# Attention followed by two dense layers on one Trainium2 core: decoding of the weights at another rate and on another DMA queue, token splits two slices a step, two output buffers, earlier first loads

## The chip, the cores and the metric

The kernel runs on one core of one Trainium2 chip. The metric is the device time of one execution in microseconds (us). TensorE is PE in the profile (PEld is its weight load), VectorE is DVE, ScalarE is ACT, GpSimd is POOL and SyncE is SP; SP only issues DMAs here.

## The reference

Batch 4, 12 heads, 448 positions, head size 64; the weights of the dense layers arrive as float64.

```python
scores = scale * q @ k.T                          # per head
scores = einsum('bhij,hg->bgij', scores, w_pre)   # heads mixed
attn = softmax(scores)                            # over the last axis
attn = einsum('bhij,hg->bgij', attn, w_post)      # heads mixed again
x = (attn @ v).transpose(0, 2, 1, 3).reshape(1792, 768)
h = x @ w_in                                      # 768 x 2048
g = where(h > 0, h, exp(min(h, 0)) - 1)
out = g @ w_out                                   # 2048 x 768
```

## The kernel before

**Attention.** Each batch is cut into 4 blocks of query positions; a block is 9 or 12 tiles of 10 positions by 12 heads (120 rows). The program is written in 92 steps `j` of up to two tiles each. In step `j` PE makes the scores of step `j+2` (tile `s`, L208), on some steps two head pairs of `q·k` for a block ahead (tile `qk`, L189; copied to `st` and sent by SP into `raw`), on some steps two head pairs of attention times values for a finished block (L259), and then the second mixing of heads of step `j` (tile `t`, L234). DVE takes the maximum `nm` (L210), the inverse sum `rz` (L220, L221), half of the `st` copies and the output copy `x` (L271); ACT makes the exponential `p` (L212) and copies `t` to `at` (L245); POOL scales the mixing matrix `wz` (L225). The results of L259 and of L234 share two PSUM banks, so the second `t` of a step has to wait until the copy `x` has emptied the bank that L259 used. A block's `x` is collected in one buffer (`xp`, one buffer) and stored to DRAM by SP after its third copy (`xd<-x`, L275).

**Decoding the weights.** `Weights.run` is a generator over 48 pieces of 128x512 weights, 24 for each layer. A piece is loaded (`w<-in`, 512 KB, L53), made into float32 by four DVE instructions (L67, L70, L76, L79 into `c`) and one ACT square (`sq`, L74, beside L70; L79 needs it), and stored to DRAM scratch (`s<-c`, L83). One call of `dec.step` goes on to the next `yield`, so a piece takes four steps; the store of a piece, the load of the piece after the next and L67 of the next come in one step. There are two `w`, two `c` and one `sq` buffers. Loads and stores are all issued by POOL.

**The dense layers.** `Moe` runs over two halves of the tokens (two chunks of 448 each, `u` = 0 and 1). The first layer has 16 slices `f` of 128 outputs: per slice and chunk 18 matmuls (L446) into `h`, then `elu`: DVE L454, ACT exponential and tanh (L456, L457), DVE L459 and L460. `keep` splits the result `g` into a high part on ACT (`gh`, L464) and a low part on POOL (`gl`, L465). The second layer has 6 row blocks `m` of two jobs `e`, each 48 matmuls (L514). Every slice and job first loads its weights from scratch (`load_w`, SP, two ahead, three buffers) and splits the next slice's (`split_w`: ACT `hi`, L395, then POOL `lo`, L396). The tokens are split in the same way: ACT `xh` (L408) and DVE `xl` (L409).

**Where decoding stands.** In attention one or two steps from `j = 6` on, in the first half's first layer one step per slice (at `u = 0`), in its second layer eight per job until the pieces are done. All engines run their instructions in the order in which the program was written; nothing reorders them.

Of the kernel before, what the change touches and what calls it, by code (L numbers as in the profile page):

```python
# [27 lines left out]
NC = DM // 128  # L28
PW = 512
EPS = 1e-9  # L30
LATE = 6


def f32(ap):
    return ap.bitcast(F32)
# [71 lines left out]
def attention(ctx, tc, qd, kd, vd, wpre, wpost, xd, dec, moe):  # L107
    nc = tc.nc
# [5 lines left out]
    def pool(name, on=ctx, side="left", **kw):  # L114
        return on.enter_context(tc.tile_pool(name=name, side=side, **kw))
# [3 lines left out]
    small = pool("small", bufs=5)  # L119
    atp = pool("at", bufs=2)  # L120
    vp = pool("v", bufs=NP + 2)
    xp = pool("x", bufs=1)
    rawp = pool("raw", bufs=2)
    kp = pool("kp", op_ctx, "right", bufs=NP + 1)
    qp = pool("qp", op_ctx, "right", bufs=2)
# [17 lines left out]
    N = len(steps)  # L143
# [30 lines left out]
    def load_v(b, hp):  # L174
        vs[b, hp] = vp.tile([128, NJ, 128], F32, tag="v", name="v")[:CJ]
        nc.gpsimd.dma_start(out=vs[b, hp], in_=vd[b, hp])
# [129 lines left out]
    def plan(j, f):  # L306
        work.setdefault(max(j, -LOOK), []).append(f)

    for n in range(1, NBL):
        b, i = blocks[n]  # L310
# [11 lines left out]
    for n in range(NBL):  # L322
        b, i = blocks[n]
# [4 lines left out]
                for hp in (2 * u, 2 * u + 1):  # L328
                    plan(j + 1, lambda b=b + 1, hp=hp: load_v(b, hp))
    for hp in range(NP):  # L330
        plan(hp + 2, lambda hp=hp: load_v(0, hp))

    sc, nz = {}, {}
    for j in range(-LOOK, N + 3):
        if j == N - 7:
            op_ctx.close()
            moe.begin()
        if j == N:
            moe.first()
        if 0 <= j + LOOK < N:  # L340
            sc[j + LOOK] = scores(*steps[j + LOOK])
        for n, u in units.get(j, ()):
            got = [qk(n, hp) for hp in (2 * u, 2 * u + 1)]
            for w in range(2):
                keep_qk(n, 2 * u + w, got[w])
        if j + LOOK - 1 in sc:
            nz[j + LOOK - 1] = norm(*sc.pop(j + LOOK - 1))
        for n, u in avs.get(j, ()):
            for w in range(2):
                av(n, 2 * u + w)  # L350
            keep_av(n, u)
        if j in nz:
            keep_post(*steps[j], post(nz.pop(j)))
        if LATE <= j < N:
            dec.step(1 + (j % 3 == 0))
        for f in work.get(j, ()):
            f()
        if N - 5 <= j < N:
            moe.ahead(j - (N - 5))


class Moe:


    def __init__(self, ctx, tc, xd, s1, s2, dec, outT):
        self.ctx, self.tc, self.nc = ctx, tc, tc.nc
        self.xd, self.dec, self.outT = xd, dec, outT

        self.jobs = [(s, lo, n) for half in range(2)
                     for s, lo, n in [(s1, f * NC, NC) for f in range(NF)]  # L370
                     + [(s2, 8 * e, 8) for e in range(2 * NC)]]
        self.w, self.x, self.banks = {}, {}, 0

    def pool(self, name, side="left", **kw):
        return self.ctx.enter_context(self.tc.tile_pool(name=name, side=side, reuse_waits="tile", **kw))
# [27 lines left out]
            self.nc.sync.dma_start(out=f32(xl[:, :, i0:i0 + m]), in_=self.xd[c][i][:, :, :m])  # L403
        self.x[c] = xh, xl

    def split_x(self, c, k):
        xh, xl = self.x[c]
        self.nc.scalar.copy(xh[:, k, :], f32(xl[:, k, :]))  # L408
        self.nc.vector.tensor_sub(xl[:, k, :], f32(xl[:, k, :]), f32(xh[:, k, :]))  # L409

    def begin(self):
# [4 lines left out]
        self.load_w(0)  # L418
        self.load_x(1)
        self.load_w(1)  # L420

    def ahead(self, step):
        if step < 4:
            for k in range(3):
                self.split_x(step // 2, step % 2 * 3 + k)
        if 1 <= step <= 2:
            self.split_w(step - 1)

    def first(self):
        self.h = [self.up(0, u) for u in range(2)]  # L430
# [16 lines left out]
                n += 1  # L447
        return h

    def elu(self, h, decode):  # L450
        nc = self.nc

        g = self.ep.tile([128, S], F32, tag="g", name="g", bufs=3)
        nc.vector.tensor_scalar_min(g, h, 0.0)  # L454
        e = self.ep.tile([128, S], F32, tag="e", name="e")
        nc.scalar.activation(e, g, AF.Exp)  # L456
        nc.scalar.activation(g, g, AF.Tanh, scale=0.5)  # L457
        self.dec.step(decode)
        nc.vector.scalar_tensor_tensor(g, e, 1.0, g, op0=ALU.add, op1=ALU.mult)  # L459
        nc.vector.tensor_max(g, g, h)  # L460
        return g
# [4 lines left out]

    def run(self):
        nc = self.nc
        self.ep = self.pool("ep", bufs=2)
        gp = self.pool("g", bufs=1)  # L470
        op = self.pool("op", bufs=2)
        self.ps.append(self.pool("ps1", bufs=1, space=PSUM))
        self.gh = [gp.tile([128, 2, S], F32R, name=f"gh{f}") for f in range(NF)]
        self.gl = [gp.tile([128, 2, S], F32R, name=f"gl{f}") for f in range(NF)]
        i = 0
        for half in range(2):
            last = None
            for f in range(NF):
                self.load_w(i + 2)
                if i:  # L480
                    self.split_w(i + 1)
                for u in range(2):
                    g = self.elu(self.up(i, 2 * half + u) if i else self.h[u], 1 - u)
                    if last:
                        self.keep(*last)
                    last = g, f, u
                del self.w[i]
                i += 1
            for m in range(NC):
                y = [self.bank("y") for u in range(2)]  # L490
                for e in range(2):
                    self.load_w(i + 2)
                    self.split_w(i + 1)
                    if last:
                        self.keep(*last)
                        last = None
                    if half == 0:
                        if m == e == 0:
                            self.load_x(2)
                            self.load_x(3)  # L500
                        if m > 1:
                            for k in range(3):
                                t = (m - 2) * 6 + e * 3 + k
                                if t < 2 * NC:
                                    self.split_x(2 + t // NC, t % NC)
                        self.dec.step(8)
                    wh, wl = self.w.pop(i)
                    i += 1
                    for u in range(2):
                        for k in range(8):  # L510
                            f = e * 8 + k
                            ks = slice(k * 128, (k + 1) * 128)
                            for n, (w, g) in enumerate(((wh, self.gh), (wl, self.gh), (wh, self.gl))):
                                nc.tensor.matmul(  # L514
                                    y[u], w[:, ks], g[f][:, u, :],
                                    start=f == 0 and n == 0, stop=f == NF - 1 and n == 2)
                for u in range(2):
                    c = 2 * half + u
                    o = op.tile([128, S], F32, tag="o", name="o")
                    nc.scalar.copy(o, y[u])  # L520
                    nc.sync.dma_start(out=self.outT[m * 128:(m + 1) * 128, c * S:(c + 1) * S], in_=o)
# [46 lines left out]
```

## Time and profile before

| what | value |
|---|---|
| median of 3 runs | 992.41 us (986.24 to 999.28) |
| the profiled execution | 990.38 us |
| its span, first to last instruction | 988.6 us |
| PE busy | 931.9 us (94%) |
| DVE / ACT / POOL busy | 531.7 / 471.3 / 453.7 us |
| mean granted TensorE clock | 0.981 |
| DMA | 136.30 MB, mean 138 GB/s |

The profiled execution spends 1.8 us outside its span. A busy share is a mean over stages with different limits: attention lies at 0 to 488 us, the first half's two layers at 488 to 621 and 621 to 753, the second half at 753 to 985. What PE waits for is therefore looked up stage by stage.

### The profile page before, as it was taken

The numbers are of one execution on the slowest core, as the hardware profiler recorded it, in microseconds if no ns is written. First come the engines' busy times: TensorE is split into PE (matmuls) and PEld (weight loads), VectorE is DVE, ScalarE is ACT, GpSimd is POOL, SyncE is SP. The second block draws the span as 40 slices with busy tenths as digits, with TensorE's granted clock in tenths as the row PEclk, the third lists the DMA queues.
The fourth block names the chain that finished last, engine by engine and source line by source line (L and its number), as shares of the span: only waits on it lengthen the run. The fifth ranks groups of instructions, "written<-read, shape, count | busy, mean of one in ns | idle before, by whom it ended". The sixth has DMA issues, their size and how long they took to land.

```text
span 988.6 us, 17106 instructions
## 1 busy us (share of the span) xinstructions
PE 931.9 (94%) x6216; PEld 771.9 (78%) x6216; DVE 531.7 (54%) x957; ACT 471.3 (48%) x988; POOL 453.7 (46%) x496
## 2 busy tenths in 40 slices
PE   4979999899999899999799999998899999999998
PEld 1657777677777677777688888887799999999997
DVE  3647666576667566765558888766611555410000
ACT  3746666556556555665535554423322555532111
POOL 2347446564457444543435555543341556543210
PEclk8989999999999999999999999999999999999999
DMA  5566456664677456757112222855532121212220
GB/s 169 174 193 214 137 182 197 199 188 138 189 224 217 125 156 189 227 169 218 63 64 89 82 86 85 225 189 188 189 117 67 50 64 48 69 58 92 74 80 29
DMA packets 76633, 136.30 MB, mean 138 GB/s; under 512 B 22894, under 2 KB 51890, under 8 KB 76550
## 3 DMA queue, kind: packets, MB, share of 16 engines
q1 hardware_dynamic: 60598, 80.41, 26.1%
q0 software_dynamic: 15408, 53.89, 17.8%
q8 instruction: 50, 0.82, 0.3%
q10 hardware_dynamic: 544, 0.92, 0.2%
q14 instruction: 33, 0.27, 0.1%
HBM read 72.86 MB, written 23.62 MB: 98 GB/s over the span
## 4 chain that ended last, share of the span: by engine, by line
PE 65%; DVE 14%; DMA 11%; issue 5%; ACT 3%; POOL 1%; SPq 1%; ACTq 0%; DVEq 0%; POOLq 0%
PE y L514 16%; PE h L446 13%; PE t L234 13%; PE s L208 12%; PE t L259 6%; PE qk L189 6%; DMA xd<-x 6%; DVE g L459 3%; DMA w<-in 3%; DVE c L79 2%; DVE g L454 2%; DVE xl L409 2%; DVE c L70 1%; DVE c L76 1%; DVE c L67 1%
## 5 line engine op out<-in xcount | busy, mean ns | idle before, releaser
L225 POOL TENSOR_SCALAR wz<-wb,rz 120x120 f32<-120x120 f32 x180 | 127.5, 716 | 182.2 <-DVE rz L221 159.5
L234 PEld LDWEIGHTS t<-wz,p 120*112 120x112 f32 x1440 | 159.3, 178 | 41.5 <-issue 31.7
L234 PE MATMUL t<-wz,p 120*112 120x120 f32 x1440 | 171.1, 271 | 14.9 <-DVE x L271 14.1
L396 POOL TENSOR_TENSOR lo<-lo,hi 128x768 fp32r<-128x768 f32 (+1 forms) x56 | 116.8, 2085 | 125.8 <-ACT hi L395 125.8
L208 PE MATMUL s<-raw,wa 120*120 120x448 f32 x360 | 156.4, 557 | 14.8 <-DMA raw<-st 7.8
L210 DVE TENSOR_REDUCE nm<-s 120x1 f32<-120x448 f32 x180 | 111.8, 624 | 96.8 <-PE s L208 86.9
L212 ACT ACTIVATE p<-s,nm 120x448 f32<-120x448 f32 x180 | 114.2, 635 | 85.6 <-DVE nm L210 81.1
L514 PE MATMUL y<-gh,lo 128*128 128x448 f32 x384 | 142.2, 370 | 9.2 <-POOL lo L396 9.2
L446 PE MATMUL h<-xh,lo 128*128 128x448 f32 x384 | 141.9, 370 | 6.6 <-POOL lo L396 6.6
L245 ACT COPY at<-t 112x480 f32<-112x480 f32 x180 | 96.4, 560 | 104.6 <-PE t L234 104.2
L514 PE MATMUL y<-gh,hi 128*128 128x448 f32 x384 | 141.2, 368 | 0.2
L446 PE MATMUL h<-xh,hi 128*128 128x448 f32 x384 | 141.2, 368 | 0.0
L514 PE MATMUL y<-gl,hi 128*128 128x448 f32 x384 | 141.2, 368 | 0.0
L446 PE MATMUL h<-xl,hi 128*128 128x448 f32 x384 | 140.8, 367 | 0.0
L465 POOL TENSOR_TENSOR gl<-g,gh 128x448 fp32r<-128x448 f32 x64 | 77.0, 1204 | 125.8 <-ACT gh L464 125.5
L208 PEld LDWEIGHTS s<-raw,wa 120*120 120x120 f32 x360 | 60.4, 188 | 51.7 <-issue 43.4
L456 ACT ACTIVATE e<-g 128x448 f32<-128x448 f32 x64 | 37.0, 579 | 123.7 <-DVE g L454 123.7
L459 DVE SCALAR_TENSOR_TENSOR g<-e,g 128x448 f32<-128x448 f32 x64 | 55.4, 865 | 63.6 <-ACT g L457 63.6
L259 PEld LDWEIGHTS t<-at,v 112*64 112x64 f32 x1536 | 74.2, 136 | 18.4 <-issue 13.7
L514 PEld LDWEIGHTS y<-gh,lo 128*128 128x128 f32 x384 | 73.4, 191 | 16.9 <-POOL lo L396 11.9
L259 PE MATMUL t<-at,v 112*64 112x120 f32 (+1 forms) x1536 | 84.1, 262 | 1.4 <-ACT at L245 1.4
L446 PEld LDWEIGHTS h<-xh,lo 128*128 128x128 f32 x384 | 72.4, 189 | 16.4 <-POOL lo L396 10.7
(49 smaller groups left out, 1255.7 us busy)
## 6 DMA issues: line engine op xcount, KB each, us to landing
raw<-st SPq DMA_DIRECT2D x144, 210.0 KB
w<-in POOLq DMA_DIRECT2D x48, 512.0 KB, 5.4
lo<-s SPq DMA_DIRECT2D x80, 256.0 KB
s<-c POOLq DMA_DIRECT2D x48, 256.0 KB, 3.5
raw<-st SPq DMA_DIRECT2D x42, 157.5 KB
q<-in POOLq DMA_DIRECT2D x15, 360.0 KB, 5.8
v<-in POOLq DMA_DIRECT2D x24, 224.0 KB, 5.2
out<-o SPq DMA_DIRECT2D x24, 224.0 KB
```

The source lines that it names most:

```text
L208: nc.tensor.matmul(ps[:RH, :S], wa, raws[n][:RH, t, :], start=True, stop=True)
L210: nc.vector.tensor_reduce(nm, ps[:RH, :S], op=ALU.max, axis=AX.X, negate=True)
L212: nc.scalar.activation(p, ps[:RH, :S], AF.Exp, bias=nm, scale=1.0, accum_out=z[:, i:i + 1])
L225: nc.gpsimd.tensor_scalar_mul(wz, wb, rz[:, i:i + 1])
L234: nc.tensor.matmul(ps[:CJ, c * RH:(c + 1) * RH], p[:, c * CJ:(c + 1) * CJ], wz, start=True, stop=True,)
L245: nc.scalar.copy(ats[n][:, :, t, :], ps[:CJ, :NJ * RH].rearrange("p (c n) -> p c n", c=NJ))
L259: nc.tensor.matmul(ps[hh * 64:(hh + 1) * 64, w * m:(w + 1) * m].rearrange("p (t r) -> p t r", r=R), vs[blocks[n][0], hp][:, c, hh * 64:(hh ...
L396: self.nc.gpsimd.tensor_sub(lo_, f32(lo_), f32(hi_))
L446: self.nc.tensor.matmul(h, w[:, ks], x[:, k, :], start=n == 0, stop=n == 3 * NC - 1)
L459: nc.vector.scalar_tensor_tensor(g, e, 1.0, g, op0=ALU.add, op1=ALU.mult)
L465: self.nc.gpsimd.tensor_sub(self.gl[f][:, u, :], g, f32(self.gh[f][:, u, :]))
L514: nc.tensor.matmul(y[u], w[:, ks], g[f][:, u, :], start=f == 0 and n == 0, stop=f == NF - 1 and n == 2)
```

## The change

The decoding starts at step 12 instead of 6, runs alternately one and two steps instead of one, one, two, and stops six steps before attention's end. In the first layer it takes a step for each of the two chunks of a slice instead of one per slice, in the second layer seven steps a job instead of eight (and whatever is left in the last row block); from the dense layers on its DMAs are issued by SP instead of POOL. The token split is cut in two calls, the high parts (`high_x`, ACT) and one step later the low parts (`low_x`, DVE), two slices of 128 rows at a time instead of three. The first loads of the dense layers are written 10 steps before attention's end instead of 7. `x` gets a second buffer. The values of the first batch are loaded two head pairs at a time at steps 4, 6 and 8 instead of one at each of steps 2 to 7.

```diff
-LATE = 6
+LATE = 12
...
-    xp = pool("x", bufs=1)
+    xp = pool("x", bufs=2)
...
     for hp in range(NP):
-        plan(hp + 2, lambda hp=hp: load_v(0, hp))
+        plan(hp // 2 * 2 + 4, lambda hp=hp: load_v(0, hp))
...
-        if j == N - 7:
+        if j == N - 10:
             op_ctx.close()
             moe.begin()
         if j == N:
+            moe.low_x(2 * NC - 2)
             moe.first()
...
+        if N - 5 <= j < N:
+            moe.low_x(2 * (j - N + 5))
         for n, u in avs.get(j, ()):
...
-        if LATE <= j < N:
-            dec.step(1 + (j % 3 == 0))
+        if LATE <= j < N - 6:
+            dec.step(1 + j % 2)
         for f in work.get(j, ()):
             f()
-        if N - 5 <= j < N:
-            moe.ahead(j - (N - 5))
+        if N - 6 <= j < N:
+            moe.high_x(2 * (j - N + 6))
+        if N - 4 <= j < N - 2:
+            moe.split_w(j - N + 4)
...
+    def high_x(self, t, n=2):
+        for t in range(t, t + n):
+            xh, xl = self.x[self.c0 + t // NC]
+            self.nc.scalar.copy(xh[:, t % NC, :], f32(xl[:, t % NC, :]))
+
+    def low_x(self, t, n=2):
+        for t in range(t, t + n):
+            xh, xl = self.x[self.c0 + t // NC]
+            r = xl[:, t % NC, :]
+            self.nc.vector.tensor_sub(r, f32(r), f32(xh[:, t % NC, :]))
...
-        self.dec.step(decode)
+        self.dec.step()
...
     def run(self):
         nc = self.nc
+        self.dec.queue = nc.sync
...
-                    g = self.elu(self.up(i, 2 * half + u) if i else self.h[u], 1 - u)
+                    g = self.elu(self.up(i, 2 * half + u) if i else self.h[u])
...
                         if m == e == 0:
+                            self.c0 = 2
                             self.load_x(2)
                             self.load_x(3)
-                        if m > 1:
-                            for k in range(3):
-                                t = (m - 2) * 6 + e * 3 + k
-                                if t < 2 * NC:
-                                    self.split_x(2 + t // NC, t % NC)
-                        self.dec.step(8)
+                        t = ((m - 2) * 2 + e) * 2
+                        if 2 <= t < 2 * NC + 2:
+                            self.low_x(t - 2)
+                        if 0 <= t < 2 * NC:
+                            self.high_x(t)
+                        self.dec.step(7 if m < NC - 1 else 64)
```

How the instructions stand on DVE over two slices of the first half's first layer, from a slice whose `u = 0` carries L79 on; `g` is the activation, `c` a piece being decoded. Before:

```order
L454 TENSOR_SCALAR g<-h 128x448
L79 SCALAR_TENSOR_TENSOR c<-sq,c 128x512
L459 SCALAR_TENSOR_TENSOR g<-e,g 128x448
L460 TENSOR_TENSOR g<-g,h 128x448
L454 TENSOR_SCALAR g<-h 128x448
L459 SCALAR_TENSOR_TENSOR g<-e,g 128x448
L460 TENSOR_TENSOR g<-g,h 128x448
L454 TENSOR_SCALAR g<-h 128x448
L67 TENSOR_SCALAR c<-w 128x512
```

In the changed kernel the lines of `elu` are five higher:

```order
L459 TENSOR_SCALAR g<-h 128x448
L76 SCALAR_TENSOR_TENSOR c<-w,c 128x512
L464 SCALAR_TENSOR_TENSOR g<-e,g 128x448
L465 TENSOR_TENSOR g<-g,h 128x448
L459 TENSOR_SCALAR g<-h 128x448
L79 SCALAR_TENSOR_TENSOR c<-sq,c 128x512
L464 SCALAR_TENSOR_TENSOR g<-e,g 128x448
L465 TENSOR_TENSOR g<-g,h 128x448
L459 TENSOR_SCALAR g<-h 128x448
L67 TENSOR_SCALAR c<-w 128x512
```

A decoding instruction now stands in both chunks of each slice, between the first and the second instruction of `elu`; L76 and L67 take turns at `u = 0`, L79 and L70 at `u = 1`.

POOL around the start of the first half's second layer, before; `lo` is the weight split of the coming job, `s` the scratch of a piece:

```order
L396 TENSOR_TENSOR lo<-lo,hi 128x1024
L465 TENSOR_TENSOR gl_6054<-g,gh_6038 128x448
L83 DMA s_8_105<-c 128x512
L53 DMA w<-in 128x1024
L83 DMA s_9_106<-c 128x512
L53 DMA w<-in 128x1024
L396 TENSOR_TENSOR lo<-lo,hi 128x1024
```

In the changed kernel POOL has only `gl` and `lo` there, and these stand on SP, among the loads of that layer's weights (`lo<-s`) and of the second half's tokens (`xl<-xd`):

```order
L393 DMA lo<-s_4_101 128x512
L393 DMA lo<-s_5_102 128x512
L408 DMA xl<-xd_0_65 128x6x90
...
L408 DMA xl<-xd_3_72 128x6x118
L83 DMA s_11_108<-c 128x512
L53 DMA w<-in 128x1024
L83 DMA s_12_109<-c 128x512
L53 DMA w<-in 128x1024
L393 DMA lo<-s_6_103 128x512
```

The stores and loads of the decoding have left POOL's row of splits and stand behind the eight token loads on SP, ahead of the next job's weights.

DVE at attention's end, from the fifth-last step's output copy on. Before:

```order
L271 COPY x<-t 128x240
L79 SCALAR_TENSOR_TENSOR c<-sq,c 128x512
L67 TENSOR_SCALAR c<-w 128x512
L409 TENSOR_TENSOR xl<-xl,xh 128x448 x3
L210 TENSOR_REDUCE nm<-s 120x1 x2
L220 TENSOR_SCALAR rz<-z 120x2
L221 RECIPROCAL rz<-rz 120x2
L70 SCALAR_TENSOR_TENSOR c<-w,c 128x512
L409 TENSOR_TENSOR xl<-xl,xh 128x448 x3
```

In the changed kernel, from the inverse sum ahead of that copy on:

```order
L221 RECIPROCAL rz<-rz 120x2
L421 TENSOR_TENSOR xl<-xl,xh 128x448 x2
L271 COPY x<-t 128x240
L210 TENSOR_REDUCE nm<-s 120x1 x2
L220 TENSOR_SCALAR rz<-z 120x2
L221 RECIPROCAL rz<-rz 120x2
L421 TENSOR_TENSOR xl<-xl,xh 128x448 x2
L210 TENSOR_REDUCE nm<-s 120x1 x2
```

The decoding instructions are gone from these steps, and two low parts of tokens stand ahead of the output copy where three stood behind it.

## Rows read from the trace of the kernel before

**Rows 1.** Busy time by stage: the stretch and its length, then for each engine busy us and (x instructions), the granted clock of PE, the DMA share, and GB/s.

```profile
0.00:100.00 100.00, 80.17 (x564) 53.87 (x566) 56.26 (x119) 53.79 (x124) 47.77 (x70) 0.91 0.61 188
100.00:458.00 358.00, 348.44 (x3052) 259.83 (x3049) 229.75 (x514) 218.91 (x519) 182.94 (x255) 0.99 0.60 183
458.00:488.00 30.00, 22.12 (x206) 17.76 (x205) 19.72 (x41) 18.62 (x42) 13.86 (x16) 0.98 0.32 106
488.00:621.00 133.00, 126.40 (x673) 113.00 (x672) 98.68 (x110) 62.16 (x110) 65.36 (x52) 0.99 0.27 82
621.00:753.00 132.00, 122.64 (x578) 111.40 (x577) 67.17 (x80) 36.26 (x58) 50.84 (x46) 0.96 0.56 174
753.00:985.00 232.00, 232.00 (x1153) 216.08 (x1151) 60.11 (x96) 81.00 (x135) 92.94 (x59) 1.00 0.19 64
```

**Rows 2.** Who waited for whom: us in total, times, longest us. The first row is DVE's over the whole span; then PE's in 100 to 460 us, in 460 to 490 (four rows), in 500 to 621 and in 621 to 753.

```profile
DVE x L271 <- DMA xd<-x: 19.3, 8, 4.0
...
PE t L234 <- DVE x L271: 9.6, 7, 2.8
...
PE t L234 <- DVE x L271: 4.5, 3, 2.2
PE t L259 <- ACT at L245: 1.4, 1, 1.4
PE s L208 <- ACT p L212: 1.1, 1, 1.1
PE t L234 <- POOL wz L225: 0.8, 1, 0.8
...
PE h L446 <- POOL lo L396: 6.6, 11, 1.1
...
PE y L514 <- POOL lo L396: 9.2, 7, 2.0
```

**Rows 3.** Instructions in order of time: start us, duration us, engine and line, then in brackets the idle time of the engine before it and what ended it. One output copy on DVE, and PE behind it.

```profile
178.11 0.34 DVE L271 COPY x<-t 128x180 f32<-128x180 f32 x1 [3.79 <-DMA xd<-x]
...
178.60 1.04 PE L234 MATMUL t<-wz,p 120*112 120x120 f32 x8 [2.85 <-DVE x L271]
```

**Rows 4.** Busy time in two of the stretches in which PE's clock was at half, columns as in rows 1; the others are 326.7 to 330.1, 487.1 to 490.5, 623.6 to 627.0, 688.5 to 691.9 and 702.1 to 705.5 us, each 3.4 us at 0.50.

```profile
63.80:70.70 6.90, 3.04 (x4) 1.12 (x4) 4.06 (x8) 3.25 (x8) 4.32 (x6) 0.51 0.47 167
179.90:183.30 3.40, 3.40 (x11) 2.12 (x10) 1.59 (x5) 1.35 (x4) 1.94 (x2) 0.50 0.61 203
```

**Rows 5.** In order of time, the first decoding instruction on DVE, and PE.

```profile
65.39 0.43 DVE L67 TENSOR_SCALAR c<-w 128x512 int32<-128x512 int32 x1 [8.21 <-DMA w<-in]
...
67.66 3.24 PE L208 MATMUL s<-raw,wa 120*120 120x448 f32 x4 [5.91 <-ACT p L212]
```

**Rows 6.** PE's first attention times values, in order of time; then the landing of a value load (issued at 51.2 us, in step 4's place) and of the 23 loads of pieces issued from 95 to 426 us, from issue to landing.

```profile
55.33 1.46 PE L259 MATMUL t<-at,v 112*64 112x90 f32 x32
...
DMA to landing us min/median/max: 6.2/6.2/6.2
...
DMA to landing us min/median/max: 4.2/6.5/8.6
```

**Rows 7.** In order of time, PE in the last steps of attention, two of its waits.

```profile
465.79 1.05 PE L234 MATMUL t<-wz,p 120*112 120x120 f32 x8 [1.63 <-DVE x L271]
...
477.75 2.83 PE L234 MATMUL t<-wz,p 120*112 120x120 f32 x24 [2.16 <-DVE x L271]
```

**Rows 8.** In order of time, the first half's first layer: DVE over one slice and the first half of the next, then POOL.

```profile
540.56 2.28 DVE L79 SCALAR_TENSOR_TENSOR c<-sq,c 128x512 f32<-128x512 f32 x1
542.77 1.58 DVE L459 SCALAR_TENSOR_TENSOR g<-e,g 128x448 f32<-128x448 f32 x1
...
544.92 0.62 DVE L454 TENSOR_SCALAR g<-h 128x448 f32<-128x448 f32 x1
546.85 0.62 DVE L459 SCALAR_TENSOR_TENSOR g<-e,g 128x448 f32<-128x448 f32 x1 [1.31 <-ACT g L457]
...
548.05 0.62 DVE L454 TENSOR_SCALAR g<-h 128x448 f32<-128x448 f32 x1
...
553.60 0.62 DVE L454 TENSOR_SCALAR g<-h 128x448 f32<-128x448 f32 x1
...
542.46 1.40 POOL L465 TENSOR_TENSOR gl<-g,gh 128x448 fp32r<-128x448 f32 x1 [0.17 <-ACT gh L464]
```

**Rows 9.** In order of time, the first half's second layer: a load of a piece and a weight split on POOL, ACT, DVE (the low parts of three token slices as one row); last the 14 loads of pieces of that layer, with the first and last start, and their landing.

```profile
658.12 0.53 POOL L53 DMA_DIRECT2D w<-in  x1
662.93 2.43 POOL L396 TENSOR_TENSOR lo<-lo,hi 128x1024 fp32r<-128x1024 f32 x1 [4.28 <-ACT hi L395]
...
661.23 0.68 ACT L74 ACTIVATE sq<-w 128x512 f32<-128x512 f32 x1 [7.75 <-DMA w<-in]
661.81 1.04 ACT L395 CAST hi<-lo 128x1024 fp32r<-128x1024 f32 x1
...
661.71 0.69 DVE L70 SCALAR_TENSOR_TENSOR c<-w,c 128x512 int32<-128x512 int32 x1
...
686.38 3.49 DVE L409 TENSOR_TENSOR xl<-xl,xh 128x448 fp32r<-128x448 f32 x3 [0.97 <-ACT xh L408]
...
L53 POOL DMA_DIRECT2D w<-in x14: 533/533/536, 634.1 to 708.6; - x14
...
DMA to landing us min/median/max: 4.3/4.9/5.9
```

More of the change, by code (lines that the diff above doesn't have):

```diff
@@ L371, in __init__ @@
                      + [(s2, 8 * e, 8) for e in range(2 * NC)]]
-        self.w, self.x, self.banks = {}, {}, 0
+        self.w, self.x, self.c0, self.banks = {}, {}, 0, 0
     def pool(self, name, side="left", **kw):
@@ L404, in load_x @@
         self.x[c] = xh, xl
[L406 to L409, printed above, removed]
+    def high_x(self, t, n=2):
[7 more added lines that the diff above has]
+            self.nc.vector.tensor_sub(r, f32(r), f32(xh[:, t % NC, :]))
     def begin(self):
@@ L420, in begin @@
         self.load_w(1)
-    def ahead(self, step):
-        if step < 4:
-            for k in range(3):
-                self.split_x(step // 2, step % 2 * 3 + k)
-        if 1 <= step <= 2:
-            self.split_w(step - 1)
     def first(self):
@@ L448, in up, with elu @@
         return h
-    def elu(self, h, decode):
+    def elu(self, h):
         nc = self.nc
@@ L498, in run @@
                         if m == e == 0:
+                            self.c0 = 2
                             self.load_x(2)
                             self.load_x(3)
-                        if m > 1:
-                            for k in range(3):
-                                t = (m - 2) * 6 + e * 3 + k
-                                if t < 2 * NC:
-                                    self.split_x(2 + t // NC, t % NC)
-                        self.dec.step(8)
+                        t = ((m - 2) * 2 + e) * 2
[4 more added lines that the diff above has]
+                        self.dec.step(7 if m < NC - 1 else 64)
                     wh, wl = self.w.pop(i)
```

## The prediction

> **What bounds the kernel now.** I read the stages first, then PE's waits in each, then the instructions around the largest. PE is the bound nearly everywhere [rows 1]: it is busy 348 of 358 us in the middle of attention and all 232 us of the second half. There 1153 matmuls take 232 us, 0.201 us each, which is the floor of a dense matmul: a slice of the first layer (36) needs 7.25 us, a job of the second (48) 9.66 us. So only idle time of PE and time at half clock can be won. Five places have some. In attention's middle PE waits 9.6 us for the output copy `x` [rows 2], and that copy had itself waited for the store `xd<-x`, 19.3 us in 8 waits. At the start PE stands 5.91 us because DVE, in order, stood 8.21 us at the first piece of weights [rows 5]. In 460 to 490 us it waits 7.8 us in six pieces [rows 2]. In the first half's layers it waits for POOL's `lo`, 6.6 and 9.2 us [rows 2], and at 621 to 753 us the granted clock is 0.96 [rows 1]. The larger waits are followed by 3.4 us at 0.50, the lower level of 1.2 GHz [rows 4]; each such stretch costs 1.7 us beside the wait. The second half has nothing to win. The sum is made against the profiled 990.38 us (988.6 of span and 1.8 around it), 2 us under the median.
>
> **Second `x` buffer.** Seven of the eight DVE waits lie in blocks where the store of the block before had not landed when its buffer was to be refilled, one of them just ahead of the last steps. With two buffers the store waited for is a whole block older, six steps of some 5 us (92 in 488), against waits of at most 4.0 us [rows 2, 3]: they all go. PE's share is at most 9.6 us in seven pieces and 1.63 us at 465.79 [rows 2, 7], 11.2 us, and two half-clock stretches, at 179.9 and 326.7 us [rows 4], 3.4 us: 14.6 us. What is late next is seen in the steps without such a wait, in which PE shows none from 100 to 460 us. I take **-13**; ends -14.6 and -7 (half of the waits turning into waits for `nm` or `rz`).
>
> **Start of decoding.** Before, the step that issued the first load also held the first L67, so DVE waited the whole landing. Now step 12 issues the load and step 13 uses it, a step of some 5 us later. With the later landings of 4.2 to 8.6, median 6.5 us [rows 6], DVE waits about 1.5 us, at most 3.6. Of the 8.21 us of before PE felt 5.91, so it had 2.3 us in hand: residue 0 to 1.3 us, taken as 0.5. Saved are 5.91 and, of the 3.04 us busy at half clock, 1.5 [rows 4, 5]: 7.4 us. But the values come later. The load in step 4's place was issued at 51.2 us and landed after 6.2 us [rows 6]; that place now holds the first two head pairs, the first landing at 57.4 and the second one transfer of 224 KB later (1.2 us at 188 GB/s, rows 1), at 58.6, and PE wants them at 55.33 and half of its 1.46 us later [rows 6]: it stands about 2.5 us. Steps 6 and 8 load for steps 8 and 10 in the same manner, behind a `ql` or `kl` on POOL; with fewer transfers around, the piece's loads being gone from there, they cost 0 to 2 and 0 to 1 us. Together +3.5, ends 1 and 7. The start is worth -7.4 + 0.5 + 3.5, **-3.5**; ends -7 and +1.
>
> **End of attention.** Without the store's wait there are 7.8 - 1.6 = 6.2 us of waits and the 1.7 us of half clock behind them. They come from DVE: three low parts and a decoding instruction a step, and the weight split on POOL, which holds up `rz` and `wz` (2.16 us, rows 7). Decoding leaves; two low parts instead of three remain, but now ahead of the output copy that frees PE's bank, 1.2 us on three steps; both weight splits remain. I take half, **-4**; ends -8 and +1. The first loads three steps earlier gain nothing by themselves, since no wait of PE or ACT for them is in these rows; they wait on SP for the last `raw` stores, and nothing is queued behind them there until the next `xd<-x`. The decoding done by attention's end is 111 steps against 115 (before 86 + 29, now 74 + 37).
>
> **First layer, first half.** A slice takes 8.0 us (from the L454 some 0.5 us ahead of L79 to the L454 at 548.05), not 7.25, and it is DVE that sets it: its instructions run with one gap only [rows 8]. At `u = 0` the decoding instruction runs into POOL's `lo` (2.28 us) and L459 into `gl` (1.58), 4.9 us for the half; at `u = 1` DVE waits 1.31 us for ACT's tanh, 3.1 us for the half. The added step falls into this gap: POOL's `gl` ended at 543.86, and an undisturbed decoding instruction takes 0.69 us [rows 9]. So 16 more steps cost nothing as long as POOL is idle there. What POOL no longer issues saves some 0.7 us on every fourth slice (5.55 us from 548.05 to 553.60 against 4.9): -2.6. The square `sq` now stands at `u = 1` on every second slice, ahead of `gh`, `hi` and so `lo`, 0.68 us each on ACT, at most 8 x 0.68 = 5.4, of which I take 3.6, since `lo` then meets DVE at another point. **+1**; ends -3 and +5. SP's store now waits there for `c`, and what is queued behind it is weights wanted two slices later.
>
> **Second layer, first half.** 132 us against a floor of 12 x 9.66 = 115.9: 16 us lost. The loop: ACT's square waits for a piece's load (7.75 us idle) and holds `hi` behind it, POOL's `lo` follows, PE waits [rows 9]. With 8 steps a job there are two loads a job, each issued only after the last L79: landing 4.9 us, four instructions 2.7 us (0.43 and three of 0.69, with their gaps), one of them held by `lo` for some 2 us, store and load issue 1.1 us, so 10.7 us a job; with the three `xl` in between (3.49 us) 14 us. Now 51 steps remain instead of 63 (16 went into the first layer's gaps), 7 a job, 1.75 pieces: 10.7 x 0.875 = 9.4 us, and two `xl` whose high part was made a job before add 1.2 us in two or three jobs, which the lead of two jobs hides. The pace is then PE's 9.66 us. The first job's loss, 1.8 us of waiting for its longer `lo` and 1.7 us of half clock, stays. **-12**; ends -16 and 0.
>
> Sum: -13 - 3.5 - 4 + 1 - 12 = -31.5, so **959 us**.
>
> **The rivals.** (1) *The step at `u = 1` meets POOL after all.* `gl` ends 1.6 us before that step's place, and the square shifts it by 0.68; if it shifted past, both halves of a slice would be as long as the first, 9.8 us: 16 x 1.8 = +28, 986 us. With halves of 5.55 us, the longest seen [rows 8], it is 16 x 3.1 = +49, **1007 us, slower than before**. For it: DVE is the bound there. Against: POOL lost work. It decides once POOL is over 1.6 us late. 0.08 and 0.03. The Trainium skill (SBUF — State Buffer, Who interferes with whom) has DVE's and GpSimd's shared port as a lock held for a whole instruction, whoever comes first; by that rule the gap is free only while POOL rests, as the 2.28 us beside 0.69 agree. (2) *SP's queue.* The loads of the second half's tokens, 8 transfers of together 2.75 MB, now stand ahead of the pieces' loads; at some 200 GB/s (174 in the mean of the stage, rows 1) that is 13 us. Before, the first such load was issued at 634.1 us, 13 us into the layer, and landed near 640 [rows 9], so the queue may well be empty by then. If the pieces do come 13 us later than that, a job still has 9.66 us for 3.5 us of `hi` and `lo`; some 7 us reach PE, with a half clock 9: 968 us, 0.1. The Trainium skill (DMA: Bandwidth & Descriptors, Queues, rings and completion order) says that an engine takes turns between queue rows but works one row's ring in order; by that rule the full 13 us would be queued, where POOL's own row shared with them. No row here shows a piece's load on SP. (3) *The copies keep waiting*, if the stores, not the buffer, are what is late: 959 + 13 = 972. The waits end at a landing of the block before, which speaks against it. 0.04.
>
> **How the numbers follow.** Forecast 0.75, the three rivals 0.11, 0.1 and 0.04. All five terms at their good ends would give 941, at their bad ends 991; as unrelated errors (1.6, 3.5, 4, 4 and 4 one way, 6, 4.5, 5, 4 and 12 the other, squares added) they give 951 and 975. With rivals 2 and 3 inside and rival 1 outside, and the good side widened for a better first layer, the range is 945 to 976. 2% of 992.4 is 20 us, about what a measurement here tells from no change, so faster means below 972.6: 0.83. Same 0.14, slower 0.03 (rival 1's long form).
>
> **What would show it.** DVE's waits for `xd<-x` gone and no half clock near 180 and 327 us; a wait of PE for values near 55 to 58 us; no 8 us wait at the first piece; a slice of the first layer still at 8 us with decoding in both halves; in the second layer jobs at 9.7 us after the first, and no `hi` behind a late square. Wrong would be slices of 9 us or more, and jobs 1 to 3 waiting for pieces on SP.

## The result, and the profile after

The changed kernel takes 949.74 us (median; 947.24 to 958.08), the kernel before in the same session 995.85 (986.24 to 1002.01): a ratio of 0.958, 95% interval 0.947 to 0.969. The forecast was 959 us. The profiled execution took 947.56 us with a span of 945.8; before it was 990.38 and 988.6. The matmuls are the same, and PE's busy share rose to 97%.

The page's head, the engines' busy time, PE's granted clock in 40 slices, and the chain that ended last, which now stays on PE for 81% of the span (65% before):

```profile
span 945.8 us, 17070 instructions
...
PE 915.8 (97%) x6216; PEld 764.4 (81%) x6216; DVE 528.7 (56%) x957; ACT 470.5 (50%) x988; POOL 435.6 (46%) x456
...
PEclk8999999999999999999999999999999999999999
...
PE 81%; DVE 8%; DMA 3%; issue 3%; ACT 3%; POOL 1%; ACTq 0%; POOLq 0%; DVEq 0%
```

The stages, columns as in [rows 1]: start, attention's middle and end, first layer and second layer of the first half, second half.

```profile
0.00:100.00 100.00, 81.76 (x606) 55.85 (x606) 51.38 (x115) 54.30 (x127) 44.56 (x67) 0.95 0.56 172
100.00:437.00 337.00, 335.85 (x2956) 250.76 (x2954) 235.55 (x515) 215.21 (x511) 184.06 (x255) 1.00 0.65 198
437.00:466.40 29.40, 26.09 (x258) 21.09 (x257) 17.24 (x38) 20.22 (x46) 14.29 (x16) 1.00 0.41 121
466.40:595.00 128.60, 124.78 (x675) 112.47 (x675) 102.89 (x127) 66.29 (x117) 66.68 (x45) 1.00 0.33 104
595.00:710.20 115.20, 115.20 (x578) 108.13 (x577) 61.55 (x69) 32.93 (x52) 33.08 (x15) 1.00 0.57 179
710.20:942.20 232.00, 232.00 (x1153) 216.10 (x1151) 60.09 (x96) 80.99 (x135) 92.95 (x59) 1.00 0.19 64
```

Beside [rows 1] the middle's idle time of PE went from 10 us to 1.2, the second layer's from 9.4 to none, and the granted clock is 1.00 from 100 us on. Cut at the first matmul of each layer and at the end of the last matmul, the stages are:

| | attention | first layer | second layer | second half |
|---|---|---|---|---|
| before, us | 487.6 | 133.2 | 132.1 | 232.1 |
| after, us | 466.4 | 128.6 | 115.2 | 232.1 |
| difference | -21.2 | -4.6 | -16.9 | 0 |

PE's waits, as in [rows 2]: in 50 to 100 us; in 100 to 440; in 440 to 466.4 (two rows); in 480 to 595. In 595 to 710 us there is none, and DVE's waits for `xd<-x` are gone from the whole span.

```profile
PE t L259 <- DMA v<-in: 4.0, 3, 2.1
...
PE t L234 <- DVE x L271: 1.1, 3, 0.5
...
PE t L234 <- POOL wz L225: 2.3, 2, 1.3
PE t L259 <- ACT at L245: 1.0, 1, 1.0
...
PE h L451 <- POOL lo L401: 3.6, 6, 1.1
```

At the start, in order of time: the wait for the piece on DVE that stood at 8.21 us [rows 5], and PE's three waits for values.

```profile
96.27 0.43 DVE L67 TENSOR_SCALAR c<-w 128x512 int32<-128x512 int32 x1 [2.36 <-DMA w<-in]
...
57.51 0.84 PE L259 MATMUL t<-at,v 112*64 112x90 f32 x16 [2.10 <-DMA v<-in]
58.74 0.84 PE L259 MATMUL t<-at,v 112*64 112x90 f32 x16 [0.40 <-DMA v<-in]
...
78.27 1.58 PE L259 MATMUL t<-at,v 112*64 112x90 f32 x32 [1.53 <-DMA v<-in]
```

DVE in the first layer, over one slice and most of the next, as in [rows 8]: the decoding instruction and the second instruction of `elu` (L464; L459 before) of each chunk. At `u = 1` both are undisturbed, 0.68 and 0.63 us.

```profile
531.74 2.02 DVE L67 TENSOR_SCALAR c<-w 128x512 int32<-128x512 int32 x1
533.68 1.59 DVE L464 SCALAR_TENSOR_TENSOR g<-e,g 128x448 f32<-128x448 f32 x1
...
536.38 0.68 DVE L70 SCALAR_TENSOR_TENSOR c<-w,c 128x512 int32<-128x512 int32 x1
537.78 0.63 DVE L464 SCALAR_TENSOR_TENSOR g<-e,g 128x448 f32<-128x448 f32 x1 [0.72 <-ACT g L462]
...
539.51 1.03 DVE L76 SCALAR_TENSOR_TENSOR c<-w,c 128x512 int32<-128x512 int32 x1
...
543.84 0.68 DVE L79 SCALAR_TENSOR_TENSOR c<-sq,c 128x512 f32<-128x512 f32 x1
```

In the second layer, SP's load of a piece, and ACT's square that waits for it, with `hi` behind, which [rows 9] had as the loop:

```profile
605.99 0.38 SPq L53 DMA_DIRECT2D w<-in  x1
...
612.28 0.68 ACT L74 ACTIVATE sq<-w 128x512 f32<-128x512 f32 x1 [5.87 <-DMA w<-in]
...
616.73 1.07 ACT L400 CAST hi<-lo 128x1024 fp32r<-128x1024 f32 x1
```

ACT still waits 5.87 us there, but PE no longer feels it: all jobs take 9.6 us, where before they took 9.6 to 14.0.

### The profile page after: what moved, and what is told of

It reads as the page before. It is cut to its first block, busy times and chain, and to the rows that moved or that the text cites. A ratio compares the mean times of both kernels' runs of the same rounds, so it can differ in the third digit from the quotient of the medians.

```text
span 945.8 us, 17070 instructions
## 1 busy us (share of the span) xinstructions
PE 915.8 (97%) x6216; PEld 764.4 (81%) x6216; DVE 528.7 (56%) x957; ACT 470.5 (50%) x988; POOL 435.6 (46%) x456
## 4 chain that ended last, share of the span: by engine, by line
PE 81%; DVE 8%; DMA 3%; issue 3%; ACT 3%; POOL 1%; ACTq 0%; POOLq 0%; DVEq 0%
PE y L521 24%; PE t L234 15%; PE h L451 14%; PE s L208 14%; PE t L259 7%; PE qk L189 7%; DVE g L464 3%; DVE g L459 2%; DVE c L67 1%; DMA v<-in 1%; ACT e L461 1%; ACT g L462 1%; POOL wz L225 1%; DMA raw<-st 1%; DMA w<-in 1%
## 5 line engine op out<-in xcount | busy, mean ns | idle before, releaser
L401 POOL TENSOR_TENSOR lo<-lo,hi 128x768 fp32r<-128x768 f32 (+1 forms) x56 | 121.0, 2160 | 152.7 <-ACT hi L400 150.7
L234 PEld LDWEIGHTS t<-wz,p 120*112 120x112 f32 x1440 | 157.3, 177 | 28.5 <-issue 22.1
L234 PE MATMUL t<-wz,p 120*112 120x120 f32 x1440 | 168.4, 269 | 3.5 <-POOL wz L225 2.3
L210 DVE TENSOR_REDUCE nm<-s 120x1 f32<-120x448 f32 x180 | 112.1, 624 | 92.7 <-PE s L208 81.3
L208 PE MATMUL s<-raw,wa 120*120 120x448 f32 x360 | 152.4, 545 | 8.0 <-DMA raw<-st 8.0
L521 PE MATMUL y<-gh,hi 128*128 128x448 f32 x384 | 139.2, 362 | 0.0
L521 PE MATMUL y<-gh,lo 128*128 128x448 f32 x384 | 139.2, 362 | 0.0
L521 PE MATMUL y<-gl,hi 128*128 128x448 f32 x384 | 139.2, 362 | 0.0
L464 DVE SCALAR_TENSOR_TENSOR g<-e,g 128x448 f32<-128x448 f32 x64 | 56.3, 879 | 56.7 <-ACT g L462 56.7
L451 PEld LDWEIGHTS h<-xh,hi 128*128 128x128 f32 x384 | 72.1, 188 | 5.9 <-issue 0.2
```

The lines of the kernel that those rows point to most:

```text
L208: nc.tensor.matmul(ps[:RH, :S], wa, raws[n][:RH, t, :], start=True, stop=True)
L210: nc.vector.tensor_reduce(nm, ps[:RH, :S], op=ALU.max, axis=AX.X, negate=True)
L234: nc.tensor.matmul(ps[:CJ, c * RH:(c + 1) * RH], p[:, c * CJ:(c + 1) * CJ], wz, start=True, stop=True,)
L401: self.nc.gpsimd.tensor_sub(lo_, f32(lo_), f32(hi_))
L451: self.nc.tensor.matmul(h, w[:, ks], x[:, k, :], start=n == 0, stop=n == 3 * NC - 1)
L521: nc.tensor.matmul(y[u], w[:, ks], g[f][:, u, :], start=f == 0 and n == 0, stop=f == NF - 1 and n == 2)
```

## The experiments

Matmuls of the second half have no wait in any run, yet in some executions they come 0.207 us apart instead of 0.201, at a granted clock of 1.00 (last section). This alone adds 6 us to that half, so parts are compared by the stages of the profiled execution, and it is said where the longer step is in them. Within attention the same instruction is compared from trace to trace, the maximum `nm` (L210) of a tile: there are 180 in each, and in the changed kernel the 61st starts at 169.4 us and the 176th at 445.4, before at 171.2 and 461.4. So of the 21.2 us that attention gained, 1.8 were there at the 61st, 14.2 came between the two, and 5.2 at the end.

**One `x` buffer again.**

```diff
-    xp = pool("x", bufs=2)
+    xp = pool("x", bufs=1)
```

> The changed kernel with one output buffer again. Theory (the buffer): DVE waits for the landing of the store xd<-x come back, about 8 of 1 to 4 us, PE feels 10 to 15 us of them with the half-clock stretches, so the first layer starts at 476 to 481 us instead of 466.4, and the whole is 11 to 15 us longer than the changed kernel (959 to 964 us). Rival (the other parts, above all the moved transfers, let the stores land in time): first layer at 466 to 469 us, whole within 3 us of the changed kernel.

Measured: 964.14 us (956.79 to 973.43), ratio to the kernel before 0.976, interval 0.968 to 0.983. Attention 475.5 us, 9.1 longer; all other stages as after. DVE's wait over the span, and PE's in 50 to 500 us:

```profile
DVE x L271 <- DMA xd<-x: 12.4, 7, 3.3
...
PE t L234 <- DVE x L271: 8.2, 8, 2.4
```

The waits of [rows 2] return and PE pays 8.2 us for them against 1.1 after, 7.1 of the 9.1 us; 1.7 us are a stretch at the lower level, 1.2 GHz, after the wait for values, which does not depend on `x`. By the maxima, 6.6 us are lost between the 61st and the 176th. The mechanism holds; its size here is a little over half of what I had.

**The second buffer alone, in the kernel before.** The diff is that of the change (`bufs=1` to `bufs=2`), nothing else.

> The kernel before with the second output buffer as the only change. Theory (the buffer was worth what the waits before showed): DVE's eight waits for xd<-x vanish, first layer starts at 473 to 476 us instead of 487.6, the dense layers as before (133 and 132 us). Rival (worth no more than undoing it in the changed kernel showed, some 7 us, the rest being taken by other waits): first layer at 479 to 482 us.

Measured: 985.39 us (one run), attention 477.2, 10.4 us shorter. DVE's waits for the store are gone, but in 50 to 480 us PE has others:

```profile
PE s L208 <- ACT p L212: 8.1, 4, 5.6
PE t L234 <- DVE x L271: 3.4, 3, 2.2
PE s L208 <- DMA raw<-st: 2.6, 1, 2.6
```

5.6 of the first row is the first piece of weights, as before. The 2.6 us for `raw` are new, and 2.9 of the 3.4 us for `x` stand at attention's end, with no wait for a store in them. So the stage fell between the two expectations: some of the gain is taken by other waits. By the maxima, 9.3 of the 14.2 us between the 61st and the 176th are gained and 1.4 at the end; the first layer is 131.9 us, 1.3 shorter than before, since the half-clock stretch behind the last waits, at 487.1 us before, now lies inside attention, at 467.1.

**Decoding's DMAs back on POOL.**

```diff
-        self.dec.queue = nc.sync
```

> The changed kernel with the decoding's DMAs left on POOL in the dense layers. Theory (the rate did it): the first half's second layer stays at 115 to 118 us (115.2 in the changed kernel, 132 before), its first layer grows from 128.6 by 2 to 5 us, since POOL again issues 1.1 us of DMAs per piece; whole 3 to 8 us longer. Rival (the queue did it): the second layer goes back to 124 us or more, whole 10 to 17 us longer.

Measured: 958.54 us (954.06 to 967.84), ratio 0.974, interval 0.966 to 0.982. First layer 135.4 us, 6.8 longer; second layer 115.8, 0.6 longer. PE's waits in the first layer (after: 3.6 us) and in the second, then POOL and DVE in a slice with a store and a load:

```profile
PE h L451 <- POOL lo L401: 9.8, 7, 2.0
...
PE y L520 <- POOL lo L401: 0.3, 1, 0.3
...
538.07 1.86 POOL L401 TENSOR_TENSOR lo<-lo,hi 128x768 fp32r<-128x768 f32 x1
539.86 0.59 POOL L83 DMA_DIRECT2D s<-c  x1
540.45 0.54 POOL L53 DMA_DIRECT2D w<-in  x1
541.00 1.17 POOL L470 TENSOR_TENSOR gl<-g,gh 128x448 fp32r<-128x448 f32 x1
...
540.12 2.54 DVE L464 SCALAR_TENSOR_TENSOR g<-e,g 128x448 f32<-128x448 f32 x1
```

The two issues take 1.13 us between `lo` and `gl`; the L464 beside them lasts until `gl` is over, 2.54 us, where after has 1.59. Every second slice grows from 7.8 to 8.7 us. (A half-clock stretch of 3.4 us at 501.9, behind the longest of these waits, is in it.) At the new rate the queue is thus worth 6.8 us to the first layer. The second layer does not need it: seven steps a job stay within PE's pace with POOL's issues too.

**The old rate.** One step a slice in the first layer, eight a job in the second, the queue still SP.

```diff
-        self.dec.step()
+        self.dec.step(decode)
...
-                    g = self.elu(self.up(i, 2 * half + u) if i else self.h[u])
+                    g = self.elu(self.up(i, 2 * half + u) if i else self.h[u], 1 - u)
...
-                        self.dec.step(7 if m < NC - 1 else 64)
+                        self.dec.step(8)
```

> The changed kernel with the old rate in the dense layers: one decoding step per slice of the first layer (at u = 0), eight per job of the second; everything else, SP's queue too, as changed. Theory (the rate did it): the second layer goes back to 124 to 131 us, the first stays within 3 us of 128.6; whole 8 to 15 us longer. Rival (the queue or the two-slice token split did it): second layer at most 118 us, whole within 4 us.

Measured: 951.45 us (949.04 to 961.28), ratio 0.965, interval 0.960 to 0.970. First layer 129.1, second 119.7 us, some 2.8 of it from matmuls 0.207 us apart from about 630 us on. The only wait of PE for the second layer:

```profile
PE y L521 <- POOL lo L401: 1.0, 1, 1.0
```

It stands in the first job; behind that, eight steps a job also fit into PE's 9.66 us if SP issues the loads. My reason for the second layer's gain, seven instead of eight, is enough by itself (the experiment before) but not needed.

**Old rate and POOL's queue together.** Both diffs above.

> The changed kernel with both the old rate in the dense layers (one step per slice, eight per job) and the decoding's DMAs on POOL there; of the changes to the second layer only the two-slice token split stays. With either one alone undone that layer lost under 2 us. Theory (rate and queue each break the loop, so both have to be undone): second layer 121 to 128 us, with waits of PE for lo in most jobs; first layer 130 to 136. Rival (the token split was the cause): second layer at most 118 us.

Measured: 971.11 us (one run); first layer 131.8, second 127.3 us, part of the latter by 0.207 us a matmul. PE's waits in 600 to 727 us:

```profile
PE y L520 <- POOL lo L401: 6.3, 6, 2.1
PE y L520 <- ACT hi L400: 0.4, 1, 0.4
```

The loop returns, with jobs of up to 13.7 us and a half-clock stretch at 676.3 us. Each of the two edits alone breaks it; only without both does PE wait. PE's waits are 6.7 us against 9.2 [rows 2], and there is one half-clock stretch against three (623.6, 688.5 and 702.1 us [rows 4]). Whether the token split two slices at a time made this difference no run tried by itself. The first layer shows what the queue is worth at the old rate: 131.8 us with POOL, 129.1 with SP in the experiment before, every fourth slice 8.7 us instead of 7.8.

**Values one a step again.**

```diff
-        plan(hp // 2 * 2 + 4, lambda hp=hp: load_v(0, hp))
+        plan(hp + 2, lambda hp=hp: load_v(0, hp))
```

> The changed kernel with the first batch's values loaded one head pair a step from step 2 on, as before. Theory: PE's three waits for values (2.1, 0.4 and 1.5 us) vanish, the first layer starts at 462 to 463 us instead of 466.4, whole 3 to 4 us shorter. Rival (the wait only moves, to the first pieces or the next scores): first layer at 465 to 467 us, whole within 2 us.

Measured: 944.99 us (943.55 to 956.81), ratio 0.961, interval 0.953 to 0.970. No wait for values is left, but attention is 465.1 us, only 1.3 shorter than after. That is not the price of the changed loading. From the 17th maximum (54.0 us in the changed kernel) to the 29th (86.4) this version gains 4.6 us, and the two below that load the values in the same way gain 4.6 and 4.5: about the 4.0 us of waits. The rest of the stage gave it back. The first wait for `raw`, over at 23 us and so ahead of the first load of values (44.3 us), took 9.0 us instead of 8.0; it lies anywhere from 7.5 to 9.4 us in the traces. One of 0.87 us for `raw` appeared at 403.8. Waits of 1.3 to 1.7 us for `raw` near 182 to 188 us stand in three other versions, in one with the values one a step and in two with the values as changed, so they are not tied to this edit; the changed kernel's trace has none.

**The piece used a step earlier.** The first load and its first use fall into one step again.

```diff
-LATE = 12
+LATE = 13
```

> The changed kernel with decoding from step 13 instead of 12, so that the first load and the first L67 stand in one step, as they did before. Theory (what cost 7.4 us at the start was that load and use stood in one step): DVE waits 5 to 8 us for the first piece near 85 to 95 us, PE 3 to 6 us behind it; first layer starts 3 to 7 us later than 466.4. Rival (the traffic at the early step 6 made the load slow, at step 13 it lands in time): PE waits under 1.5 us, first layer within 2 us of 466.4.

Measured: 952.08 us (one run), attention 471.8, 5.4 longer. DVE at the first piece, and PE behind it in 50 to 130 us:

```profile
100.22 0.43 DVE L67 TENSOR_SCALAR c<-w 128x512 int32<-128x512 int32 x1 [5.32 <-DMA w<-in]
...
PE t L234 <- DVE x L271: 2.5, 1, 2.5
```

DVE waits 5.32 us instead of 2.36 and PE 2.5 us instead of 0.4 at most. So the step between load and use is worth 2.1 us to PE. Before, with load and use in one step too, PE stood 5.91 us [rows 5]; there the load took 7.7 us to land, here 4.0. The other 3.4 us thus go with the later start, which is the rival. The rest of the 5.4 us is a stretch at the lower level at 58.2 us, after a value wait of 2.14 us, and two small waits (1.30 and 0.75 us).

**Decoding up to attention's end.**

```diff
-        if LATE <= j < N - 6:
+        if LATE <= j < N:
```

> The changed kernel with decoding going on to attention's end, as before, instead of stopping six steps ahead. Theory (half of what the end gained came from the decoding's leaving): PE's waits after the last block's scores grow from 3.2 us by 1 to 4 us, first layer 1 to 4 us later than 466.4; the dense layers start with nine more steps done and lose nothing. Rival (the token split and the second buffer were the gain): first layer within 1 us of 466.4.

Measured: 949.49 us (one run), attention 468.1. At the 176th maximum this version is 3.0 us behind the kernel after, by a half-clock stretch of 6.8 us at 57.9; at the stage's end it is 1.7 behind. PE's waits at attention's end:

```profile
PE t L234 <- ACT xh L415: 1.1, 1, 1.1
PE t L234 <- POOL wz L225: 1.1, 1, 1.1
```

That is 2.2 us with decoding there and 3.3 without it. Decoding's leaving was not the gain at the end. The first layer takes 126.5 us and the second 117.2, together the same as after.

**Two steps of decoding at `u = 1`, none at `u = 0`.**

```diff
-        self.dec.step()
+        self.dec.step(decode)
...
-                    g = self.elu(self.up(i, 2 * half + u) if i else self.h[u])
+                    g = self.elu(self.up(i, 2 * half + u) if i else self.h[u], 2 * u)
```

> The changed kernel with the two decoding steps of a slice of the first layer both at the second chunk (u = 1), none at the first. Theory (the step at u = 0 is the one that meets POOL, the gap at u = 1 is free): slices at 7.3 to 7.5 us, first layer 122 to 125 us instead of 128.6, whole 4 to 6 us shorter than the changed kernel. Rival (two instructions of together 1.4 us overfill the gap of 1.3 us, or other instructions meet POOL instead): first layer 127 us or more.

Measured: 945.35 us (942.74 to 958.05), ratio 0.953, interval 0.947 to 0.958. First layer 125.4 us, in an execution whose matmuls came 0.207 us apart there: from the fifth on every slice takes 7.44 us, which is 36 of them. PE is the bound of the layer.

**Both: values one a step and two steps at `u = 1`.** The last diff and that of the values.

> The changed kernel with the values one head pair a step and both decoding steps at u = 1. Theory: the gains add, first layer starts at 463 to 465 us and lasts 122 to 125 us, whole 937 to 941 us in an execution at the usual matmul pitch. Rival (they do not add, or e6 gains nothing): 943 us or more.

Measured: 939.21 us (937.66 to 941.03), ratio 0.948, interval 0.945 to 0.951. The first layer, and DVE in one chunk at `u = 1` and the next at `u = 0`:

```profile
465.00:588.40 123.40, 122.36 (x675) 113.06 (x674) 79.89 (x128) 66.32 (x118) 64.28 (x45) 1.00 0.34 108
...
545.45 0.41 DVE L67 TENSOR_SCALAR c<-w 128x512 int32<-128x512 int32 x1
545.90 0.69 DVE L70 SCALAR_TENSOR_TENSOR c<-w,c 128x512 int32<-128x512 int32 x1
...
548.56 0.62 DVE L459 TENSOR_SCALAR g<-h 128x448 f32<-128x448 f32 x1 [0.43 <-PE h L451]
550.50 0.87 DVE L464 SCALAR_TENSOR_TENSOR g<-e,g 128x448 f32<-128x448 f32 x1 [1.32 <-ACT g L462]
```

Slices are 7.3 us, which is 36 matmuls at 0.203, DVE now waits for PE, and PE waits 1.0 us in the whole layer. In their profiled executions, both with 0.201 us a matmul, this is 6.5 us of span better than the change (1.4 in attention, 5.2 in the first layer), and the best version that was run.

**The same, with the weight splits in attention's last two steps.**

```diff
-        if N - 4 <= j < N - 2:
-            moe.split_w(j - N + 4)
+        if N - 2 <= j < N:
+            moe.split_w(j - N + 2)
```

> The kernel of e7 with the first two weight splits of the dense layers two steps later, behind the last scaling of the mixing matrix on POOL. Theory (PE's last waits in attention, 1.3 and 1.0 us for wz and 1.0 us for at, come from POOL's lo ahead of wz): these three go, first layer starts 2 to 3.2 us earlier than in e7 (462 to 463 us), whole 936 to 938 us. Rival (the splits come too late for the first slices): first layer 1 us or more longer, whole as e7.

Measured: 947.99 us (936.73 to 949.91), ratio 0.953, interval 0.948 to 0.959. Attention 459.9 us, 5.1 shorter than in the version before; 1.8 of them were there at the 176th maximum, ahead of the moved splits. Only 0.3 us of PE's 3.3 us of waits is left at its end: these came from `lo` ahead of `wz` on POOL. But five of six executions took 946 to 950 us, and the profiled one has matmuls 0.207 us apart from 482 us on. The version gains 3.3 us at attention's end; whether it is better in all is open.

## Why the prediction was right, and where not

The forecast was some 9 us too long by the median, 11 by the profiled executions (-31.5 against -42.8 us of span). Attention as a whole came out as added up, 21.2 us against 20.5; 5.6 us are missing in the sum for the first layer and 4.9 in that for the second.

**Second `x` buffer, -13.** By rows: 11.2 us of PE's waits became 1.1, and the two half-clock stretches went, 3.4 us: -13.5. By the maxima the kernel gained 14.2 us between the 61st and the 176th. The mechanism is right, but the size is not the buffer's alone: 9.3 us of the 14.2 come with the buffer put in alone, and with all other edits and one buffer 7.6 are there already; the two overlap. Which of the other edits does it is open; the rate of decoding in attention, one and two steps in turn, was undone in no run. That -13 fits so well is in part luck.

**Start, -3.5.** The waits came where they were placed: of the 5.91 us at the first piece at most 0.4 is left, and the value waits are 2.10, 0.40 and 1.53 us, 4.0 in sum against 3.5. Their price was about right: the three versions without them gain 4.5 or 4.6 us there. By the 61st maximum the kernel was 1.8 us ahead, half of the forecast and within its ends. The reason given for the saving, a step between load and use, is worth 2.1 us; the rest goes with the later start, at which the load landed in 4.0 us instead of 7.7 (the piece used a step earlier).

**Attention's end, -4.** 6.2 us of waits became 3.3, and the half-clock stretch of 1.7 us behind them went: -4.6. By the maxima it is 5.2 ahead of the first layer. Of the reasons, "Decoding leaves" fails (one run): with decoding there the waits are no longer. "Both weight splits remain" holds: moving them took the rest. The second buffer alone gained 1.4 there. That leaves the order of the low parts, two ahead of the copy instead of three behind it, and the earlier first loads; neither was tried alone.

**First layer, +1.** Measured -4.6, of which some 1.4 is the half clock counted above: the second buffer alone, without that stretch in this layer, has 131.9 us. From there the experiments account for the rest: old rate and POOL's queue 131.8, old rate and SP's queue 129.1, new rate and SP's queue 128.6. So "-2.6" for what POOL no longer issues was right (2.7), and the added step cost nothing, as said: 0.68 us at `u = 1` beside 0.69 [rows 9]. Mis-sized was "+3.6" for the square, which did not show: the slice after a square is the fast one, 7.45 us against 7.77, since L76 takes 1.03 us at its `u = 0` where L67 takes 2.02 in the other, and PE's waits fell from 6.6 to 3.6 us. What the sum had no term for is how rate and queue hang together. At the new rate POOL's issues come on every second slice and hold DVE too, by the delayed `gl`: with them the layer takes 135.4 us, so the new rate on the old queue would have cost 3.6 us.

**Second layer, -12.** Measured -16.9, all that there was to lose. The loop "10.7 x 0.875 = 9.4" stands: seven steps a job keep up with PE on POOL's queue as well. But the sum did not say that the queue does it by itself: 10.7 less the 1.1 us of issue in it is 9.6, also under 9.66, and eight steps on SP's queue left no wait behind the first job. Only without both does the loop return. Mis-sized was "The first job's loss, 1.8 us of waiting for its longer `lo` and 1.7 us of half clock, stays": it is none of the 3.5 us. `lo` is done at 594.9 us, PE starts at 595.0. With a margin of 0.1 us this is in part luck: in three other versions PE waits 0.2 to 1.0 us there, with the old rate and POOL's queue 1.9.

By the stages the parts give -1.8 - 14.2 - 5.2 - 4.6 - 16.9 = -42.7 of the 42.8 us of span.

**The rivals.** (1) No chunk at `u = 1` met POOL: the decoding instruction there took 0.68 us in all 16 slices. The rule of the Trainium skill (SBUF — State Buffer, Who interferes with whom), one of the two engines blocked for the other's whole instruction, went with the rows: 2.02 us for L67 at `u = 0` beside `lo`, 0.41 for the same instruction at `u = 1` in the version with both edits. (2) SP's queue held a piece back, but by 1 to 2 us of the 13. The token loads, issued from 596.0 us on, moved data until 609.9 by the DMA packets of the trace. The load of a piece issued at 605.99 us moved its first data 2.6 us later, where the loads in the first layer took 1.0 to 1.5, and was used at 612.28, 6.3 us after its issue; PE did not feel it. The Trainium skill (DMA: Bandwidth & Descriptors, Queues, rings and completion order) has one ring worked in order, and the trace agrees in that the piece's data began only when the token loads were nearly through. What was too large is how much still stood ahead of the piece. (3) The copies do not wait for stores any more.

## What to carry to other kernels

In an engine that works in order, put optional work where that engine waits for another one, not beside an operation that slows it: two decoding steps in ACT's gap cost nothing, one beside POOL's splits in each slice made it 0.3 us longer on average (7.61 against 7.30). DMA issues on an engine whose results the bound engine needs cost more than their own time: 1.1 us of issue on every second slice was worth 6.8 us of the stage. An edit's worth can depend on the other edits: in the second layer either of two was enough, and in the first the new rate would have lost time on the old queue. And compare two traces at several instructions, not only at a stage's end: taking out 4.0 us of value waits gained 4.6 by 86 us, of which 1.3 were left at 466; the rest went into waits that other runs show as well.

## What the runs showed of the hardware

Matmuls of 448 columns that wait for nothing start 0.200 to 0.203 us apart in some stretches (0.201 in the mean of a half) and 0.207 in others, with the granted clock at 1.00 in both. 100 us of the second half, from 800 us on, in the version with both edits and in that with the late splits, PE busy all the time:

```profile
800.00:900.00 100.00, 100.00 (x500) 93.61 (x499) 12.69 (x20) 26.80 (x42) 35.53 (x20) 1.00 0.23 76
...
800.00:900.00 100.00, 100.00 (x485) 90.67 (x485) 14.27 (x23) 26.05 (x41) 35.52 (x20) 1.00 0.22 72
```

500 matmuls against 485. The longer step comes in spells. In the changed kernel's trace there are two, 496 to 511 and 556 to 574 us; with the late splits it lasts from 482 us to the end; with the old rate and POOL's queue it stands from 621 to 654 us and again from 699 to the end. One begins just behind a wait of PE (1.03 us, over at 481.7, with the late splits), one with no wait near it (628 us, the old rate). From the dense layers to the end it costs 12 us (2.2, 3.8 and 6.1 by stage, the late splits against both edits), which is about how far the times of one kernel lie apart, and more than several of the edits tried here are worth. Its cause stays open; no run was aimed at it.

The fall of the clock after a wait is not fixed by the wait alone: after the value wait of 2.10 us in the changed kernel the clock stayed at the upper level, 2.4 GHz, after one of 2.14 us in the same place (the piece used a step earlier) it was at the lower for 3.4 us. After 1.78 us (one `x` buffer) it fell too, after 2.27 us (old rate and POOL's queue) it did not. Small changes of time at the start are therefore worth little as evidence.
